# Later waits for loads, wide state reads and a last layer in quarters, in a block-recurrent attention and mixture-of-depths kernel

## The chip, the core and the metric

The kernel runs on one core of one Trainium2 chip. The metric is the time of one execution in microseconds on the device. TensorE (PE) multiplies matrices, VectorE (DVE) and ScalarE (ACT) work element by element, GpSimd (POOL) does small operations and issues the transfers by index, SyncE (SP) issues most other transfers. Each engine works through its own instructions in order.

## What is computed

Eight batches of x (8 heads, 512 rows, 64 columns) and a state (8 heads, 32 rows, 64 columns) attend to each other: every row of x reads the state, every row of the state reads x. The results, 544 rows of 512 columns per batch, go through a mixture of depths: a gate scores each row, and the 128 rows with the highest scores pass a two-layer network.

```python
scores = scale * x @ state.T              # 512 x 32 for each head
xread = softmax(scores) @ state           # rows 0..511 of the output
sread = softmax(scale * state @ x.T) @ x  # rows 512..543
rows = concatenate([xread, sread])        # heads side by side: (8, 544, 512)
s = rows @ w_gate
for b in range(8):
    top = the 128 rows of batch b with the largest s
    ye = maximum(rows[b, top] @ w1, 0) @ w2      # 512 -> 1024 -> 512
    out[b, top] = rows[b, top] + sigmoid(s[b, top]) * ye
```

All data is float32. The profile shows each such matrix product as two records of TensorE.

## The kernel before, in words

**Pieces and their order.** The kernel first writes its work down as 697 numbered pieces (`add`, line 143), each with an engine, a batch and the pieces that it comes after. `carry_out` (line 147) then emits them in the order of the list `ORDER` (lines 18 to 45), which sets the order on every engine at once. An entry `199/0/w04` is piece 199, its PSUM bank 0, and ahead of it 4 dummy products into bank 0 (line 163), whose results nobody reads. All waits follow from buffers and from the dependences written with `add_manual_dep`.

**One batch.** x comes in by rows (`load_x`, line 293, two transfers of 512 KB for batches 1 to 7). Batches 0 to 3 turn x on TensorE (line 411). Batches 4 to 7 also fetch it as blocks in four transfers of 256 KB (`load_x2`, line 309, "blocked x"), which VectorE turns (line 415). The scores are line 448. VectorE works out the softmax over the state (lines 467 to 496). The "read" multiplies it with the state (line 559), in two pieces per batch; each product takes 128 columns of the turned weights in batches 0 to 3 (`WIDE`, line 97) and 64 in batches 4 to 7, hence half as many products when wide. The read also delivers the gate's sums, which VectorE takes out (line 567), while ScalarE copies the rows (line 563). The state's read of x is line 621; batches 4 to 7 get its weights turned over a transfer out (`a_out`, line 587, 512 KB) and four back in (`a_in`, line 592). ScalarE copies its rows (line 627), VectorE makes the state's part of the gate (lines 679 and 689).

**The choice.** A batch's rows are stored to the output (`store_base`, line 646: 1 MB by `store_x`, 64 KB by `store_s`; batch 0 on ScalarE's queue, the others on SP's). The scores, laid out as a row (lines 700 and 703), are compared with each other on VectorE (lines 735 and 742; batches 0 to 2 count the rest on TensorE, line 772). A one-hot matrix (line 788) picks the 128 row numbers (lines 807 and 811). GpSimd then fetches these rows from the output by index ("fetch", line 816), after both stores of the batch have landed. Four to eight small operations give the sigmoid.

**The layers.** They run for the groups [0], [1, 2], [3, 4], [5, 6] and [7] (line 959): the fetched rows are turned (line 874), multiplied with w1 (line 915, "first"), rectified, multiplied with w2 (line 935, "second"), scaled and added to the fetched rows (line 938), and written back by index (`put`, line 946). Batches 6 and 7 do the second layer in two halves of 256 columns (line 929), each with an add and a put of its own; the index of a half is twice the row number plus 0 or 1 (`halved`, line 941).

**What waits behind what.** `HELD` (line 94) makes loads wait until a fetch has landed: x and blocked x of batch 4 behind fetch 0, of 5 behind fetch 2, of 6 behind fetch 3, of 7 behind fetch 4. `HELD_ST` holds batch 1's stores behind fetch 0. `behind` (line 287) writes these waits. Blocked x also comes after the scores of two batches before, and x by rows after the load before it on its queue (`chain`). `touches` (line 638) declares that transfers to the output of different batches do not depend on each other; those of one batch keep their dependence.

Of the kernel before, what the change touches and what calls it, by code (L numbers as in the profile page):

```python
# [10 lines left out]
I32 = mybir.dt.int32  # L11
AF = mybir.ActivationFunctionType
ALU = mybir.AluOpType
# [2 lines left out]


ORDER = """
0 1 2 4 17 3 6 7 8 9 19 20 10 11 31/7/w08 33/6 27/0 35/3 37/2 5 28 32 36 34 38 12 39/0/w03 114/2 40 13 14 116/6 25/5
41/0 45 15 117 26 115 46 47 42 43 16 118/7 29/6 120/2 179/3 181/5 63/4 183/0 65/1 119 121 44 66 180 64 182 24 22 21 54  # L20
500 122/1/w23 185/3 268/7 48 49 123 127 184 269 186 30 67/4 50/5 270/3 52/6 68 51 271 128 129 55/0/w07 175/5 272/4
142/7 124 125 133 71 56 53 126 57 58 273 176 143 72/6 59/0 274/4 275 335 130 73 60 131 132 74/5 144/6 76/7 177/4 75 62
77 178 61 69 145 70 83 187/4/w51 134/0 498/7 146/6 79 81 82 188 135 78 192 80 136 137 499 147 138/0 276/6 141 140 193
194 150 189 139 281 84/2 151/1 85 86 152 198 153/3 207/2 87/5/w01 155/4 209/1 89 154 88 208 156 210 282 283 90 23 91
18 162 190 161 157 160 159 158 277 211/0/w04 333/3 298/2 296/1 96/4 163/7 212 191 92 97 299 334 297 195 196 278 197
279 164 215 165 103/6 98/5 104 99 100 199/0 101 105 166/4 216/7 200 338 341 336 149 337 214 339 148 340 280 201 202
102 167 203/0 106 284 217 285 204 168 286 218/5 220/4 93 170 227 206 219 221 205 108/7 288/0 224 223 225 222 226 228/5
109 107 290 171 291 287 229 230 289 231/6 292/1 300/0 233 232 294 295 301 342 343 94 344 293 345 304 110 307/5 305/1
346/2 306 351 347 213 169 234 95 321 172 235 309/6 240/1 242/0 308 241 243 310 352 353 111 247/4 244/0 253/2 254 248
245 314 348 366 316 311 367 319 318 312 315 317 313 320 349 322 323 302 433 431 434 436 368 435 303 369 324/5 250/6  # L30
350 325 246 255 249 354 326 355 356 251 358/1 370/5 112 437 359 440 357 438 360 361 371 252 236 362/1/w01 374 375/7
363 376 439 327 113 328 237 391 403/0 377/5 379/6 365 378 380 404 364 262/7 441/2 256/5 263 264 432 501 503 373 504
372 506 505 389 238 382 388 387 390 383 381 384 386 385 446 392 393 394/6 257 265 258 259 329 447 448 461 396 462 442
173 443 444 509 510 507 508 463 397 330 174 239 502 464 405/3 445 406 395 511/0 410/6 407/3 408 465/4 449 331 516 512
452 450 451 517 518 409 466 260 531 532 606 607 609 533 608 534 453/0 411 413/4 513 454 514 266 469 455 456 515 457/0
470/5 416/7 414 417 519 520 458 612 471 521 613 522 611 610 332 398 261 486 459 460 415 412 399 418 472/5 474/4 523/0
419/6 535/7 473 475 525 526 536 479 481 478 484 485 483 524 476 480 539 527/0 540/4/w41 528 477 482 541 487 488 530
529 467 468 538 604 537 542/7 544/5/w51 543 545 614/2 489/4 420 421 422 556 400 267 552 553 551 546 555 549 554 548
547 550 557 491 558 619 559/7 490 560 620 621 561 634 401 635 615 625 616 617 423 492 562 402 493 563 425/1 426 427
568/7 570/2 428 636 605 637 569 571 618 494 622 623 429 624 572/7 575/5 573 578/4 626/0 638/6 576 628 564 629 574 639  # L40
627 642 630/0 643/7 579 644 631 632 633 577 495 565 424 659 640 641 645/2 647/6 581/3 598/5 591/0 582 584/7 646 648
580 583 496 651 649 655 653 654 656 652 650 657 658 660 661 566 662/2 585 599 592 600 593 601 586 594 663 567 666 667
497 668 664 669 595 602 665 670 430 590 683 597 603 596 690 671/4 672 587 678/3 673/4 679 674 675 676 680 681 677 682
684/4 685 686 687 691/2 692 693 694 588 688 689 589 695 696
"""


# [1 line left out]
def kernel(  # L49
# [10 lines left out]
    nc = tc.nc  # L60

    B, H, S, D = x.shape
    Ns = state.shape[2]
    Dm, F = moe_w1.shape
    SP = S + Ns
    NC = S // 128
# [25 lines left out]
    XG_BLOCKS = ()  # L92
    TURNED = (0,)
    HELD = {4: 0, 5: 2, 6: 3, 7: 4}
    HELD_ST = {1: 0}
    GATES_PE = (0, 2)
    WIDE = (0, 1, 2, 3)
    ROWS_OUT = ()
    FULL = (3, 4, 5, 6, 7)
    const = pool("const", 1)  # L100
# [2 lines left out]
    small = pool("small", 6)  # L103
# [39 lines left out]
    def add(engine, name, fn, after=(), takes=(), uses=(), b=0):  # L143
        pieces.append(Piece(engine, name, fn, after, takes, uses, b))
        return pieces[-1]
# [80 lines left out]
    after = const.tile([128, SP], F32, name="after")  # L226
# [55 lines left out]
    same_b = ident.bitcast(BF16)  # L282
    xf, p_x, last_load, x2, p_x2, p_scores = {}, {}, [], {}, {}, {}

    fetched = {}

    def behind(b, st):

        for p in fetched.get(b, ()):
            tc.add_manual_dep(st.ins, p.ins.name, mybir.DependencyInfo(mybir.DependencyClass.Sync, mybir.DependencyReason.DATA),  # L290
                              reason="transfers behind the fetch of rows")

    def load_x(b, pieces=2):
        buf = xf[b] = Buf(R_X)
        n = H // pieces
        p_x[b] = []
        for h in range(0, H, n):

            on = "ACT" if b == 0 and h + n == H else "SP"

            def go(h=h, on=on):
                queue = nc.scalar if on == "ACT" else nc.sync
                behind(HELD.get(b), queue.dma_start(out=buf.ap[:, h:h + n], in_=x[b, h:h + n].rearrange("h (p c) d -> p h c d", c=NC)))

            chain = [q for q in last_load if q.engine == on][-1:]
            p_x[b].append(add(on, "load_x", go, after=chain + list(fetched.get(HELD.get(b), ())), takes=[] if h else [buf], uses=[buf] if h else [], b=b))
            last_load.append(p_x[b][-1])

    def load_x2(b):

        buf = x2[b] = Buf(R_X2)
        p_x2[b] = []
        for w in range(2):
            for e in range(2):
                def go(w=w, e=e):
                    src = x[b].rearrange("h (s t r w) (e d) -> w e t r h s d", s=4, t=32, r=2, e=2)[w, e]
                    o = 32 * (2 * w + e)
                    behind(HELD.get(b), nc.sync.dma_start(out=buf.ap[o:o + 32], in_=src))

                p_x2[b].append(add("SP", "load_x2", go, after=[p_scores[b - 2]] + list(fetched.get(HELD.get(b), ())), takes=[] if p_x2[b] else [buf], uses=[buf] if p_x2[b] else [], b=b))  # L320

    def load(on, name, fn, uses=()):
        chain = [q for q in last_load if q.engine == on][-1:]
# [322 lines left out]
    def store_base(b, xs, tmp, p_xs, p_xt):  # L646
        on = "ACT" if b < 1 else "SP"
        queue = nc.scalar if on == "ACT" else nc.sync

        def store(st):  # L650
            touches(b, st)
            behind(HELD_ST.get(b), st)

        def x_rows():
            store(queue.dma_start(out=out[b, 0:S].rearrange("(p c) m -> p c m", c=NC), in_=xs.ap))

        def s_rows():
            dst = out[b, S:SP].rearrange("n (g q d) -> q n g d", g=2, q=4)
            store(queue.dma_start(out=dst, in_=tmp["xt"]))

        held = list(fetched.get(HELD_ST.get(b), ()))
        return [add(on, "store_x", x_rows, after=p_xs + held, uses=[xs], b=b), add(on, "store_s", s_rows, after=[p_xt] + held, b=b)]

    def by_number(b, **kw):

# [194 lines left out]
    def layers(units, number):  # L860
# [4 lines left out]
        n = at[-1]  # L865
        xg, hT = Buf(R_XG), Buf(R_HT)
# [35 lines left out]
        p_h = []  # L902
# [23 lines left out]
        for u, lo in zip(units, at):  # L926
            m, ot = u["m"], Buf(R_OT)

            parts = [slice(0, Dm // 2), slice(Dm // 2, Dm)] if u["b"] >= B - 2 else [slice(0, Dm)]
            for k, part in enumerate(parts):  # L930
                py = Buf(P_H)

# [5 lines left out]
                    nc.vector.scalar_tensor_tensor(ot.ap[0:m, part], py.ap[0:m, part], u["z"].ap[0:m, 2:3], u["xr"].ap[0:m, part],  # L938
                                                   op0=ALU.mult, op1=ALU.add)

                def halved(u=u, m=m, k=k):

                    u[k] = small.tile([128, 1], I32, name="half", bufs=4)
                    nc.gpsimd.tensor_scalar(u[k][0:m], u["idx"].ap[0:m], 2, k, op0=ALU.mult, op1=ALU.add)

                def put(u=u, m=m, ot=ot, part=part, n=len(parts), k=k):
                    ix = u["idx"].ap if n == 1 else u[k]
                    by_number(u["b"], out=flat_out.rearrange("r (n m) -> (r n) m", n=n),
                              out_offset=bass.IndirectOffsetOnAxis(ap=ix[0:m, 0:1], axis=0), in_=ot.ap[0:m, part], in_offset=None)

                p_n = [add("POOL", "halved", halved, after=[u["gate"]], uses=[u["idx"]], b=number)] if len(parts) > 1 else []

                n_parts, p = len(parts), None
                for f0 in range(0, NF, 2):
                    p = add("PE", "second_h" if n_parts > 1 else "second", lambda f0=f0, go=second_layer: go(f0), after=p_h[0:f0 // nf + 1] + [p_w2, p], takes=[] if f0 else [py], uses=[hT] + ([py] if f0 else []), b=number)
                p = add("DVE", "add_h" if n_parts > 1 else "add", add_rows, after=[p, u["gate"]], takes=[] if k else [ot], uses=[py, u["xr"], u["z"]] + ([ot] if k else []), b=number)
                add("POOL", "put", put, after=[p] + p_n, uses=[ot, u["idx"]], b=number)

    groups = [[0], [1, 2], [3, 4], [5, 6], [7]]
# [52 lines left out]
```

## Time and profile before

| What | us |
|---|---|
| median of 3 runs (200.06 to 201.47) | 201.04 |
| the profiled execution | 203.17 |
| its span, first to last instruction | 201.4 |
| TensorE busy | 189.4 |
| VectorE busy | 141.5 |
| ScalarE busy | 77.6 |
| GpSimd busy | 52.2 |
| first layer of group 0 starts | 44.34 |
| first layer of group 1 starts | 70.95 |
| last second-layer product ends | 196.58 |
| batch 1's 1 MB store issued by SP | 51.36 |
| fetch 0, 1, 2, 3, 4 issued | 38.77, 60.13, 63.74, 83.15, 100.24 |
| fetch, issue to landing: least, median, most | 3.4, 4.3, 7.2 |

The profile is of one execution. The span is shorter than the execution's own time, which has start and end around it. TensorE's records end where a model of its pipeline puts them, so durations are best taken from one start to the next. Idle time in brackets names what ended last according to the profile; where that had long been done, it was something else, often a transfer. "issue" is time in which an engine waited for nothing that the profile shows.

### The profile page before, as it was taken

To read this page: it belongs to the slowest core of one execution; us is meant where nothing else is said; L and a number is where in the kernel's file an instruction comes from. 1 tells how busy PE (TensorE), PEld (TensorE's weight loads), DVE (VectorE), ACT (ScalarE), POOL (GpSimd) and SP (SyncE) were. 2 spreads that over 40 slices of the span, in tenths; PEclk is the share of its full clock that TensorE was granted. 3 is DMA by queue.
4 is the path that set the end of the run, shared out by engine and by line. 5 is a ranking of instruction groups with operands and counts; after the bars stand their busy time and mean duration, and the time that the engine had idled before them with its cause. 6 is when DMAs were issued, how large, how long until landed. Compare 5 with 4: busy or idle time off the path is not lost.

```text
span 201.4 us, 5778 instructions
## 1 busy us (share of the span) xinstructions
PE 189.4 (94%) x2412; PEld 138.3 (69%) x2412; DVE 141.5 (70%) x343; ACT 77.6 (39%) x178; POOL 52.2 (26%) x150
## 2 busy tenths in 40 slices
PE   7999999989999799999997999999999999999990
PEld 3787677679956488874444878664468787768980
DVE  4289999999876799758997999699887039011000
ACT  2399886782543412353221452640340451000200
POOL 7020030282414300250022111024620210624042
PEclk9999999999999999999999999999999999999999
DMA  6999946039898498978999988436275051020002
GB/s 193 367 321 373 381 158 226 5 84 180 206 315 312 152 209 191 153 263 144 282 283 151 122 212 138 192 105 277 73 260 88 10 221 49 8 96 26 29 26 78
DMA packets 67218, 35.04 MB, mean 174 GB/s; under 512 B 54904, under 2 KB 63096, under 8 KB 66168
## 3 DMA queue, kind: packets, MB, share of 16 engines
q1 hardware_dynamic: 64676, 28.97, 55.8%
q0 software_dynamic: 1312, 4.20, 6.1%
q10 hardware_dynamic: 1204, 1.51, 2.1%
q8 instruction: 19, 0.31, 0.7%
q14 instruction: 7, 0.06, 0.1%
HBM read 21.56 MB, written 13.11 MB: 172 GB/s over the span
## 4 chain that ended last, share of the span: by engine, by line
PE 56%; DVE 14%; DMA 5%; issue 4%; ACT 2%; POOL 1%; POOLq 1%; DVEq 0%; ACTq 0%
PE ps L915 29%; PE ps L935 15%; PE ps L559 5%; DMA xr<-out_dram,idx 5%; DVE win L742 4%; DVE win L735 3%; PE ps L874 2%; DVE xT L415 2%; PE ps L621 1%; POOL out_dram L666 1%; PE ps L700 1%; DVE oh L788 1%; PE ps L807 1%; DVE spare L583 1%; PE ps L772 1%
## 5 line engine op out<-in xcount | busy, mean ns | idle before, releaser
L915 PE MATMUL ps<-xg,w 128*128 128x256 f32 (+1 forms) x320 | 59.0, 341 | 0.2 <-ACT xg L877 0.2
L935 PE MATMUL ps<-w,hT 128*128 128x512 f32 (+1 forms) x160 | 58.7, 513 | 0.0
L915 PEld LDWEIGHTS ps<-xg,w 128*128 128x128 f32 x320 | 50.6, 191 | 7.0 <-issue 1.4
L935 PEld LDWEIGHTS ps<-w,hT 128*128 128x128 f32 x160 | 29.3, 190 | 19.1 <-issue 17.2
L563 ACT COPY xs<-ps 128x512 f32<-128x512 f32 x32 | 17.7, 590 | 25.6 <-DVE sc L567 11.4
L666 POOL DMA_INDIRECT xr<-out_dram,idx x8 | 9.6, 1194 | 44.1 <-DVE idx L811 21.2
L938 DVE SCALAR_TENSOR_TENSOR ot<-ps,z,xr 128x512 f32<-128x512 f32 (+1 forms) x10 | 6.2, 633 | 20.6 <-PE ps L935 17.7
L735 DVE SCALAR_TENSOR_TENSOR win<-srow,sc,after 128x416 bf16<-128x416 f32 (+4 forms) x40 | 18.9, 506 | 1.9 <-ACT srow L726 1.7
L559 PE MATMUL ps<-st_v,eT 32*64 32x65 f32 (+1 forms) x768 | 18.0, 247 | 1.5 <-issue 0.8
L559 PEld LDWEIGHTS ps<-st_v,eT 32*64 32x64 f32 (+1 forms) x768 | 15.2, 149 | 6.0 <-issue 2.9
L742 DVE SCALAR_TENSOR_TENSOR win<-srow,sc,before 128x512 bf16<-128x512 f32 (+4 forms) x25 | 14.7, 588 | 4.9 <-ACT srow L724 4.5
L918 ACT ACTIVATE hT<-ps 128x512 f32<-128x512 f32 x16 | 9.4, 606 | 15.5 <-PE ps L915 15.5
L484 ACT ACTIVATE e<-e 128x1024 f32<-128x1024 f32 x8 | 8.5, 1060 | 14.7 <-DVE e L481 14.7
L506 ACT ACTIVATE a<-ps,nm 128x512 f32<-128x512 f32 x14 | 9.6, 694 | 9.5 <-DVE nm L502 6.5
L877 ACT COPY xg<-ps 128x512 f32<-128x512 f32 x8 | 4.6, 589 | 17.2 <-PE ps L874 17.1
L163 PE MATMUL ps<-ident 128*128 128x512 bf16 x30 | 9.8, 447 | 1.3 <-POOL ident masks.py:199 1.3
L756 POOL CAST aux<-sc 128x5 bf16<-128x5 f32 x8 | 2.4, 306 | 31.4 <-DVE sc L689 17.8
L415 DVE STREAM_TRANSPOSE xT<-x 128x512 f32<-128x512 f32 x16 | 10.6, 686 | 0.0
L488 DVE TENSOR_REDUCE sm<-e 128x32 f32<-128x1024 f32 x8 | 9.6, 1204 | 0.9 <-ACT e L484 0.8
L502 DVE TENSOR_REDUCE nm<-ps 128x2 f32<-128x1024 f32 x7 | 8.5, 1215 | 2.2 <-PE ps L448 2.2
L493 DVE TENSOR_TENSOR e<-e,sm 128x1024 f32<-128x1024 f32 x8 | 9.7, 1217 | 0.1
L411 PE MATMUL ps<-ident,xf 128*128 128x128 f32 x64 | 9.8, 295 | 0.0
(114 smaller groups left out, 249.4 us busy)
## 6 DMA issues: line engine op xcount, KB each, us to landing
xf<-in_x_dram SPq DMA_DIRECT2D x14, 512.0 KB, 6.0
out_dram<-xs SPq DMA_DIRECT2D x7, 1024.0 KB, 4.9
w<-in_moe_w_dram SPq DMA_DIRECT2D x2, 2048.0 KB
x<-in_x_dram SPq DMA_DIRECT2D x16, 256.0 KB, 4.4
a_d<-spare SPq DMA_DIRECT2D x4, 512.0 KB, 3.8
aT<-a_d SPq DMA_DIRECT2D x16, 128.0 KB, 3.5
out_dram<-xs ACTq DMA_DIRECT2D x1, 1024.0 KB
xf<-in_x_dram SPq DMA_DIRECT2D x3, 256.0 KB
```

Of the source, the lines that this page charges most:

```text
L163: nc.tensor.matmul(banks[:, 512 * bank:512 * (bank + 1)], same_b[:, 0:128], same_b.unsqueeze(1).to_broadcast([128, 2, 256]), start=True, s ...
L411: nc.tensor.transpose(v[:, k, r], xf[b].ap[:, 2 * pair + k, 2 * r:2 * r + 2].rearrange("p w d -> p (w d)"), ident)
L415: nc.vector.transpose(out=t.ap.rearrange("p k r t -> p r k t"), in_=x2[b].ap[:, :, 2 * pair:2 * pair + 2].rearrange("p r k s d -> p r k (s ...
L488: nc.vector.reduce_sum(out=sm, in_=e.ap, axis=AX.X)
L493: nc.vector.tensor_tensor(out=e.ap, in0=e.ap, in1=tmp["sm"].to_broadcast([128, 32, Ns]), op=ALU.mult)
L559: nc.tensor.matmul(view(o)[t, q, c - c0, g], eT.ap[r, c % 2, g, c // 2, t], st_v[r, b, g], start=True, stop=True)
L563: nc.scalar.copy(out=xs.ap[:, c].rearrange("p (g q m) -> p g q m", g=2, q=4), in_=view(o)[:, :, c - c0, :, 0:D].rearrange("p q g m -> p g ...
L666: st = nc.gpsimd.indirect_dma_start(**kw)
L735: nc.vector.scalar_tensor_tensor(wins[c].ap[0:n], srow.ap[0:n, f:SP], sc[0:n, b, c:c + 1], after[0:n, 0:SP - f], op0=ALU.is_gt, op1=ALU.mu ...
L742: nc.vector.scalar_tensor_tensor(unders[c].ap[0:n, 0:f + n], srow.ap[0:n, 0:f + n], sc[0:n, b, c:c + 1], before[0:n, S - f:S + n], op0=ALU ...
L915: nc.tensor.matmul(o, w(j), i[:, :, j] if n == 256 else i[:, 0, j], start=(j == 0), stop=(j == ND - 1))
L935: nc.tensor.matmul(py.ap[0:m, part], hT.ap[:, f, lo:lo + m], w2[:, f, part], start=(f == 0), stop=(f == NF - 1))
```

## The change

Four things are changed, and `ORDER` is a new list for the 711 pieces that result; it has 23 dummies in place of 30.

- The first two blocked pieces of x of batch 4 wait for batch 0's stores to land, and not for fetch 0. In SP's new order batch 1's 1 MB store and batch 2's 64 KB store stand between the two pieces.
- x by rows gets a table of its own (`HELD_X`): batch 4 behind fetch 2, 5 behind fetch 3, 6 and 7 behind fetch 4. It no longer comes after the load before it. Batch 3's stores wait for fetch 2.
- The reads of all eight batches are wide.
- The second layer of batch 7 is done in four quarters of 128 columns, each with its own index, add and put. Batch 6 keeps its halves.

```diff
+    HELD_X = {4: 2, 5: 3, 6: 4, 7: 4}
-    HELD_ST = {1: 0}
+    HELD_ST = {1: 0, 3: 2}
-    WIDE = (0, 1, 2, 3)
+    WIDE = (0, 1, 2, 3, 4, 5, 6, 7)
...
-    fetched = {}
+    fetched, stored, EARLY = {}, {}, 2
-    def behind(b, st):
+    def behind(b, st, of=None):
-        for p in fetched.get(b, ()):
+        for p in (fetched if of is None else of).get(b, ()):
...
-                behind(HELD.get(b), queue.dma_start(out=buf.ap[:, h:h + n], ...
+                behind(HELD_X.get(b), queue.dma_start(out=buf.ap[:, h:h + n], ...
-            p_x[b].append(add(on, "load_x", go, after=chain + list(fetched.get(HELD.get(b), ())), ...
+            p_x[b].append(add(on, "load_x", go, after=(chain if b < 4 else []) + list(fetched.get(HELD_X.get(b), ())), ...
...
+                first_two = b == 4 and len(p_x2[b]) < EARLY
-                    behind(HELD.get(b), nc.sync.dma_start(out=buf.ap[o:o + 32], in_=src))
+                    st = nc.sync.dma_start(out=buf.ap[o:o + 32], in_=src)
+                    if first_two:
+                        behind(0, st, stored)
+                    else:
+                        behind(HELD.get(b), st)
...
-            parts = [slice(0, Dm // 2), slice(Dm // 2, Dm)] if u["b"] >= B - 2 else [slice(0, Dm)]
+            n_parts = 4 if u["b"] == B - 1 else 2 if u["b"] == B - 2 else 1
+            parts = [slice(Dm * k // n_parts, Dm * (k + 1) // n_parts) for k in range(n_parts)]
...
-                    u[k] = small.tile([128, 1], I32, name="half", bufs=4)
-                    nc.gpsimd.tensor_scalar(u[k][0:m], u["idx"].ap[0:m], 2, k, op0=ALU.mult, op1=ALU.add)
+                    u[k] = small.tile([128, 1], I32, name="half", bufs=6)
+                    nc.gpsimd.tensor_scalar(u[k][0:m], u["idx"].ap[0:m], n_parts, k, op0=ALU.mult, op1=ALU.add)
```

SP's transfers after the weights, in both orders (x2 is blocked x, x is x by rows, st the 1 MB store, ss the 64 KB store, ao and ai the way out and back of the weights; the number is the batch):

```
before: x2.4 x2.4 x.4 ss.1 x.4 ss.2 x2.4 st.1 x2.4 st.2 st.3 x2.5 x.5 x2.5 x2.5 ao.4 x2.5 ss.3 ai.4 x.5 x.6
        x2.6 ss.4 x2.6 st.4 x2.6 x2.6 ao.5 x.6 ai.5 x2.7 x2.7 x2.7 ao.6 x2.7 ai.6 st.5 ss.5 ss.6 x.7 st.6 ao.7 x.7 ai.7 st.7 ss.7
after:  x2.4 st.1 ss.2 x2.4 x2.4 ss.1 x2.4 st.2 x2.5 ss.3 x.4 x2.5 x.4 x2.5 ao.4 x2.5 st.3 ai.4 x2.6 x.5
        x2.6 ss.4 x2.6 st.4 x2.6 ao.5 x.5 ai.5 x2.7 x.6 x2.7 x2.7 ao.6 x2.7 x.6 ai.6 x.7 ss.5 st.5 ss.6 st.6 ao.7 x.7 ai.7 st.7 ss.7
```

## The prediction, made before the changed kernel had run

> **What bounds the kernel now.** I read the page's busy shares first, then the 40 slices, the chain that ended last, and then the timelines of the engines and of SP's DMA queue. TensorE is busy in 94% of the span, at a granted clock of 0.999.
>
> ```profile
> PE 189.4 (94%) x2412; PEld 138.3 (69%) x2412; DVE 141.5 (70%) x343; ACT 77.6 (39%) x178; POOL 52.2 (26%) x150
> ...
> PE   7999999989999799999997999999999999999990
> ...
> DMA  6999946039898498978999988436275051020002
> ```
>
> The slices hide two different halves. Up to 44 us VectorE sets the pace (4.1 to 5.0 of each 5 us from 10 on); from 44.34, where the first layer of group 0 starts, to 196.58 PE runs with few holes. These are the holes worth naming, and the reads that the change widens (start, duration, engine; in brackets the idle time ahead):
>
> ```profile
> 57.03 1.12 PE L559 MATMUL ps<-st_v,eT 32*128 32x65 f32 x32
> 58.09 0.69 PE L772 MATMUL ps<-ones,win 128*128 128x1 bf16 x15
> ...
> 68.77 0.63 PE L874 MATMUL ps<-ident,xr 128*128 128x128 f32 x4 [1.49 <-DMA xr<-out_dram,idx]
> ...
> 86.68 0.44 PE L559 MATMUL ps<-st_v,eT 32*64 32x65 f32 x15 [0.40 <-issue]
> 87.06 1.10 PE L621 MATMUL ps<-xf,aT 128*32 128x64 f32 x64
> ...
> 88.56 0.92 PE L559 MATMUL ps<-st_v,eT 32*64 32x65 f32 x64
> 89.41 0.22 PE L686 MATMUL ps<-part_s,same_n 128*32 128x1 f32 x2
> ...
> 107.55 0.63 PE L874 MATMUL ps<-ident,xr 128*128 128x128 f32 x4 [1.07 <-DVE sm L488]
> ```
>
> From start to next start a wide read costs 1.05 us (batches 0 to 3), an undisturbed narrow one 0.85. At 107.55 the last wait is not the VectorE sum: batch 4's row fetch was issued at 100.24 and the longest fetch took 7.2 us to land, so it arrives there. The end of the kernel:
>
> ```profile
> 182.08 1.02 POOL L666 DMA_INDIRECT out_dram<-ot,half  x1 [4.69 <-issue]
> ...
> 184.80 0.97 POOL L666 DMA_INDIRECT out_dram<-ot,half  x1 [1.58 <-DMA out_dram<-ot,half]
> ...
> 189.51 7.07 PE L935 MATMUL ps<-w,hT 128*128 128x256 f32 x32
> ...
> 193.31 0.48 DVE L938 SCALAR_TENSOR_TENSOR ot<-ps,z,xr 128x256 f32<-128x256 f32 x1 [10.00 <-PE ps L935]
> 194.08 1.00 POOL L666 DMA_INDIRECT out_dram<-ot,half  x1 [8.05 <-DVE ot L938]
> ...
> 196.62 0.48 DVE L938 SCALAR_TENSOR_TENSOR ot<-ps,z,xr 128x256 f32<-128x256 f32 x1 [2.82 <-issue]
> 197.38 0.96 POOL L666 DMA_INDIRECT out_dram<-ot,half  x1 [0.90 <-DVE ot L938]
> ```
>
> The reader should see the second line: the second half of batch 6 had been ready, and its put waited for the first half's put to land, 2.72 us from issue to issue. Puts of one batch stay dependent (line 640 frees only other batches).
>
> **The change, part by part.** Sums are against the profiled span of 201.4 us. That execution took 203.17 us, 2.1 above the median of 201.04; I add the difference to the median.
>
> *Quarters.* On PE: two halves take 2 x 3.47 us (189.67 to 193.14); at 128 columns the first layer's rows give 7.14 us for 64 records, 0.112 each, so four quarters of 16 take 7.14: +0.2. On POOL: the changed program's instruction order shows each quarter's put waiting for the landing of the one before. Its PE order interleaves the quarters: quarter 0 is done 9 pieces of 0.447 us, 4.0 us, before PE's end. Add 0.1 of lag, 0.35 for a 128x128 add (estimate from 0.73 at 512 columns and 0.48 at 256), 0.27 from add to put: the first put starts 3.3 us before PE's end. The other quarters are ready every 1.3 us; the puts follow every 2.6 us. Of the 2.72 us the burst of data is some 0.4 (DMA rates of 181 to 186 us), so half the bytes save 0.1 to 0.2; bounds 2.4 (the median landing of a half) and 2.72. The last put starts 3 x 2.6 - 3.3 = 4.5 us after PE's end, where it now starts 0.8 after (197.38 against 196.58). From its start to the span's end it is 4.0 now, 0.1 less with half the bytes. **+3.6** (3.0 to 4.0). The add and the first put are hidden under PE; the rest has no cover, since nothing follows. The two more index multiplications are 0.21 each, in POOL's idle time before.
>
> The Trainium skill, "DMA: Bandwidth & Descriptors", Anatomy of one DMA, gives about 2.0 us fixed, mostly the write receipt, plus bytes over 436 GB/s. By it a 64 KB put would take 2.15 us where a half takes 2.3, and the term would be about 0.4 smaller. It speaks against quarters as the 2.72 row does: what is paid per put hardly shrinks with it.
>
> *Wide reads.* The eight narrow reads of batches 4 to 7 take, start to start, 1.82, 0.85, 1.81, 0.98, 0.85, 0.84, 0.84, 0.84: 8.83. Eight wide ones at 1.05 are 8.40: **-0.4**. This rests on the two slow ones, which stalled on "issue" (0.40 and 0.38, and slow issue around it). I take these as gone, since half of the instructions are left to issue; if they stay (2 x 0.97), the term is +1.5.
>
> The Trainium skill, "TensorEngine Tiling (Array Packing)", Available Configurations, lists eight independent tiles of 32x64 but four of 32x128, which speaks against wide reads; taken alone, with the narrow rows unstalled, it would make them dearer by 8 x 0.20 = 1.6.
>
> *Batch 4's blocked x and batch 1's store.* In SP's queue only one of the two early pieces is early: the second stands behind batch 1's store, which waits for fetch 0 (42.96), and behind the state rows of batch 2. The first moves 256 KB in 35 to 39 us, where the DMA slice is 0, ahead of fetch 0's data. What moves more is batch 1's store: before, it left SP at 51.36 behind six transfers and fetch 1 started only at 60.13, its index ready at 53.9. Now it leaves at 43, so fetch 1 starts at about 54.2 and lands at 59; batch 2's store leaves at about 55.4, lands at 60.4, fetch 2 lands at 65.3 (4.9, as now). PE comes to that row turn at 67.4: the 1.49 idle goes. Next late is the threshold count of batch 2 (VectorE ready 0.4 after PE). PE's own pieces, added up at their rows' times in the new order, come out 0.2 shorter (fewer changes of shape): **-1.3** at the start of group 1's first layer (bounds -1.5 and 0).
>
> *Holding x by rows and batch 3's store behind fetch 2.* Behind the waiting transfer SP now queues st 3, x of 4 and the blocked x of 5, ahead of batch 4's weights (a_out, a_in). Before, from fetch 2's landing (68.7) to a_out's landing (80.0) were 11.3 us for three blocked pieces, one 512 KB piece and a_out. Now another 512 KB (1.35 us at 390 GB/s, seen at 86 to 88) and 64 KB (0.4) are in it, from 65.3: 78.4. Then blocked piece four (1.6), the 1 MB store (2.7 at 60 to 63) and a_in (3.2) give 86 and 0.6 to land. PE needs a_in at 85.8. **+0.8** (0 to 2.5). Fetch 3 now also waits for that store, 83.5, and lands near 88.2; PE wants it at 88.9: hidden, by 0.7.
>
> *Fetch 4.* Its issue stays near 100.2 (store 4 lands at 99.8); one blocked piece fewer runs beside it, so I take 6.0 us to land instead of 7.2 (bounds 4.9, 7.2). PE waits 0.3 instead of 1.07: **-0.8** (-1.1 to +0.4).
>
> *Order.* Batch 1's first gate now stands behind a row copy that follows ScalarE's store issues (1.13 and 0.37): VectorE, the pace up to 44 us, loses **+0.3**. Around 130 to 142 us 0.33 idle and two dummies of 0.45 and 0.49 go, and waits of 0.7 and 0.4 for batch 6's state score and gate come: **-0.3** rounded with the earlier row turn. Seven fewer dummies elsewhere stand in waits and cost nothing.
>
> Sum: 0.2 + 3.6 - 0.4 - 1.3 + 0.8 - 0.8 + 0.3 - 0.3 = **+2.1**, 203.1 us.
>
> **Rivals.**
> A, not slower: every hole goes. From 44.34 to 196.58 PE takes 152.24 us, in it 6.5 of idle, stalls and dummies. Without them, plus 1.6 for wide against unstalled narrow reads and 0.2 for quarters: 147.5. That is -4.7, with the tail +3.6: -1.1, 199.9. For it: fetches lead by 2 us at 67. Against: DMA is full from 70 to 105. It decides once the gain before the last layer passes 3.6.
> B, faster side: the puts do not wait for each other on the chip. Then the last put starts 0.7 after PE's end, the tail term is -0.1, 199.4. With a spacing p the term is 3p - 4.2, so it decides from p below 1.9 on. Against it stands 184.80.
> C, slower: the queue behind fetch 2 is the bound. At the 184 GB/s mean of 70 to 85 us the 3.6 MB up to batch 3's store take 19.6 us from 66.5, until 86.1; fetch 3 lands at 91.2, 2.3 late, and the blocked x of 6 behind it: +4.3, 205.4. It decides when that store lands after 84.
>
> **How the numbers follow.** The forecast has 0.52, C 0.23, A 0.15, B 0.10. Predicted 203.1. Within 1% (what a measurement of this kernel can tell from no change) reaches from 199.0 to 203.05, so the forecast's own spread (201.6 to 204.6) is cut in two: slower 0.27 + 0.23 = 0.50; same 0.25 + 0.13 + 0.05 = 0.43; faster 0.02 + 0.05 = 0.07. The range of 200.0 to 205.6 takes in A's upper side and C, and leaves most of B out.
>
> **What would show it.** Quarters: four puts at the end spaced 2.4 to 2.7 us, each waiting on a DMA, the last starting over 4 us after PE's end; spaced 1.3, B. Reads of batches 4 and 5 at 1.05 without a gap; otherwise that term is wrong. No idle ahead of the second row turn near 67. A wait at L621's state read near 86, and fetch 3 landing before 89; later, C. PE ending near 195; at 192, A.

## The result, and the profile after

The changed kernel takes 213.01 us (median of 4 runs, 211.97 to 214.41), the kernel before on the same chip 201.25 (4 runs): a ratio of 1.059, 95% interval 1.050 to 1.069. The profiled execution took 214.41 us, its span is 212.6 (201.4 before). Ratios, here and below, leave out runs more than 1.5% above the fastest of their kernel; medians do not.

From the page of the changed kernel: TensorE's share and instructions, then 40 slices of 5.3 us of TensorE's busy tenths, of the granted clock and of the DMA engines.

```profile
PE 194.2 (91%) x2181; PEld 142.3 (67%) x2181; DVE 142.6 (67%) x345; ACT 78.3 (37%) x178; POOL 57.3 (27%) x156
...
PE   7997998999999999599999999998999999999910
...
PEclk9999999799999999955999999999999999999995
DMA  6999925357471799959889997743692070102000
```

The clock row was nines throughout before (mean 0.999; now 0.954). It falls in slice 8, in slices 18 and 19, and in the last, where TensorE is idle anyway. TensorE's timeline in the columns of the prediction:

```profile
46.95 3.83 PE L924 MATMUL ps<-xg,w 128*128 128x128 f32 x32
...
70.06 0.60 PE L883 MATMUL ps<-ident,xr 128*128 128x128 f32 x4
...
85.15 1.12 PE L566 MATMUL ps<-st_v,eT 32*128 32x65 f32 x32
...
90.85 1.93 PE L628 MATMUL ps<-xf,aT 128*32 128x64 f32 x64 [2.66 <-DMA aT<-a_d]
...
98.85 8.10 PE L945 MATMUL ps<-w,hT 128*128 128x512 f32 x16
...
114.04 0.60 PE L883 MATMUL ps<-ident,xr 128*128 128x128 f32 x4
```

The first layer of group 0 starts at 46.95 (44.34 before). Batch 2's row turn at 70.06 has no idle ahead, where 1.49 stood. The wide read takes 1.05 from start to next start. Then come the two things to see: batch 4's state read (L628) waits 2.66 us for its weights, and behind it, until 100.8, the clock is at 0.50: that read takes 1.93 instead of 1.10, and 16 matmuls of the second layer, of which a part falls in this time, take 8.10 instead of 7.13. Two stretches of 2 us (busy times, then granted clock, DMA share and GB/s) show hole and clock:

```profile
88.00:90.00 2.00, 0.19 (x1) 0.00 (x0) 0.17 (x1) 0.60 (x1) 0.08 (x1) 1.00 1.02 165
...
92.00:94.00 2.00, 2.00 (x55) 1.83 (x49) 0.30 (x2) 1.01 (x3) 0.00 (x0) 0.50 0.76 122
```

What kept the weights is in SP's own queue (issue time and how long issuing took): x by rows of batch 4, batch 3's store of 1 MB, and only then the weights' way in, which lands at 90.85.

```profile
72.16 2.38 SPq L304 DMA_DIRECT2D xf<-in_x_dram  x1
...
78.55 3.36 SPq L663 DMA_DIRECT2D out_dram<-xs  x1
82.28 4.21 SPq L599 DMA_DIRECT2D aT<-a_d  x4
```

The end, on TensorE, VectorE and GpSimd:

```profile
195.97 6.86 PE L945 MATMUL ps<-w,hT 128*128 128x128 f32 x60
```
```profile
199.01 0.35 DVE L948 SCALAR_TENSOR_TENSOR ot<-ps,z,xr 128x128 f32<-128x128 f32 x1 [10.07 <-PE ps L945]
...
202.88 0.35 DVE L948 SCALAR_TENSOR_TENSOR ot<-ps,z,xr 128x128 f32<-128x128 f32 x1 [0.99 <-PE ps L945]
```
```profile
199.64 1.00 POOL L675 DMA_INDIRECT out_dram<-ot,half  x1 [4.54 <-DVE ot L948]
202.75 0.96 POOL L675 DMA_INDIRECT out_dram<-ot,half  x1 [2.00 <-DMA out_dram<-ot,half]
205.76 0.96 POOL L675 DMA_INDIRECT out_dram<-ot,half  x1 [1.94 <-issue]
208.75 0.96 POOL L675 DMA_INDIRECT out_dram<-ot,half  x1 [1.91 <-issue]
```

All adds are done at 203.2; the puts go on 3.0 us apart, the last one 5.9 us after TensorE's end (0.8 before). Cut at four instructions, the two spans differ like this:

| stretch | before, us | after, us | difference |
|---|---|---|---|
| up to group 0's first layer | 44.34 | 46.95 | +2.6 |
| to group 1's first layer | 26.61 | 25.63 | -1.0 |
| to group 2's first layer | 38.18 | 43.02 | +4.8 |
| to TensorE's last matmul | 87.45 | 87.23 | -0.2 |
| to the span's end | 4.82 | 9.77 | +5.0 |

The sum is the spans' difference, 11.2 us. Both profiles are of long executions, about 2 us above the median before and 1.4 after, so the rows hold to a us or so. Three places need a cause: the start, the middle with the late weights and the half clock, and the end.

### The profile page after: what moved, and what is told of

Same layout as the page of the kernel before. It is cut to its first block, busy times and chain, and to the rows that moved or that the text cites. A ratio compares the mean times of both kernels' runs of the same rounds, so it can differ in the third digit from the quotient of the medians.

```text
span 212.6 us, 5321 instructions
## 1 busy us (share of the span) xinstructions
PE 194.2 (91%) x2181; PEld 142.3 (67%) x2181; DVE 142.6 (67%) x345; ACT 78.3 (37%) x178; POOL 57.3 (27%) x156
## 5 line engine op out<-in xcount | busy, mean ns | idle before, releaser
L945 PE MATMUL ps<-w,hT 128*128 128x512 f32 (+2 forms) x192 | 60.0, 462 | 0.0
L945 PEld LDWEIGHTS ps<-w,hT 128*128 128x128 f32 x192 | 31.0, 193 | 20.2 <-issue 19.1
L675 POOL DMA_INDIRECT xr<-out_dram,idx x8 | 9.5, 1189 | 50.5 <-DVE idx L820 44.8
L744 DVE SCALAR_TENSOR_TENSOR win<-srow,sc,after 128x544 bf16<-128x544 f32 (+4 forms) x40 | 18.9, 508 | 2.7 <-ACT srow L735 2.5
L566 PEld LDWEIGHTS ps<-st_v,eT 32*128 32x128 f32 x512 | 16.6, 194 | 4.1 <-issue 1.7
L566 PE MATMUL ps<-st_v,eT 32*128 32x65 f32 x512 | 18.8, 285 | 0.5 <-ACT xs L570 0.2
L948 DVE SCALAR_TENSOR_TENSOR ot<-ps,z,xr 128x512 f32<-128x512 f32 (+2 forms) x12 | 6.6, 557 | 17.2 <-PE ps L945 17.1
L751 DVE SCALAR_TENSOR_TENSOR win<-srow,sc,before 128x128 bf16<-128x128 f32 (+4 forms) x25 | 14.7, 589 | 3.3 <-ACT srow L733 2.9
L628 PEld LDWEIGHTS ps<-xf,aT 128*32 128x32 f32 x512 | 8.3, 117 | 5.7 <-issue 4.0
L628 PE MATMUL ps<-xf,aT 128*32 128x64 f32 x512 | 9.7, 232 | 2.7 <-DMA aT<-a_d 2.7
L675 POOL DMA_INDIRECT out_dram<-ot,half x6 | 6.0, 997 | 17.3 <-issue 10.7
```

Of the source, the lines that this page charges most:

```text
L566: nc.tensor.matmul(view(o)[t, q, c - c0, g], eT.ap[r, c % 2, g, c // 2, t], st_v[r, b, g], start=True, stop=True)
L628: nc.tensor.matmul(o2.ap[rr, D * g:D * (g + 1)], (aT[g].ap if aT else aT2.ap[:, g])[:, c, rr], xf[b].ap[:, 4 * g + q, c], start=(c == 0), ...
L675: st = nc.gpsimd.indirect_dma_start(**kw)
L744: nc.vector.scalar_tensor_tensor(wins[c].ap[0:n], srow.ap[0:n, f:SP], sc[0:n, b, c:c + 1], after[0:n, 0:SP - f], op0=ALU.is_gt, op1=ALU.mu ...
L751: nc.vector.scalar_tensor_tensor(unders[c].ap[0:n, 0:f + n], srow.ap[0:n, 0:f + n], sc[0:n, b, c:c + 1], before[0:n, S - f:S + n], op0=ALU ...
L945: nc.tensor.matmul(py.ap[0:m, part], hT.ap[:, f, lo:lo + m], w2[:, f, part], start=(f == 0), stop=(f == NF - 1))
```

## The experiments

Each kernel was run beside the kernel before on the same chip; chips differ (medians of the kernel before from 200.9 to 202.6), so the ratio is the number to compare.

| kernel | us | before, us | ratio (95%) |
|---|---|---|---|
| the changed kernel | 213.0 | 201.3 | 1.059 (1.050-1.069) |
| b1: changed, halves | 208.1 | 202.3 | 1.027 (1.019-1.034) |
| c3: changed, puts apart | 207.8 | 202.6 | 1.024 (1.018-1.030) |
| b4: before, quarters | 205.8 | 202.3 | 1.018 (1.008-1.028) |
| a2: changed, store 3 free | 210.3 | 202.1 | 1.045 (1.035-1.055) |
| b2: changed, x of 4 free | 208.5 | 202.3 | 1.029 (1.019-1.039) |
| b3: changed, both free | 208.5 | 202.3 | 1.030 (1.022-1.039) |
| a3: changed, dummies at the late read | 212.7 | 202.1 | 1.052 (1.041-1.062) |
| c2: changed, x of 4 free, halves | 203.0 | 202.6 | 1.002 (0.999-1.006) |
| e1: old order, new transfers, x of 4 free | 201.5 | 201.0 | 1.005 (1.002-1.009) |
| e2: the same, x of 4 held | 204.6 | 201.0 | 1.017 (1.011-1.022) |
| a4: changed, early dummies | 212.8 | 202.1 | 1.057 (1.048-1.066) |
| d1: before, ten dummies fewer | 202.9 | 200.9 | 1.008 (1.004-1.012) |
| c4: the same kernel as d1, 4 runs of 201.4 to 207.6 | 204.9 | 202.6 | not on record |
| d4: changed, x of 4 free, puts apart | 203.5 | 200.9 | 1.006 (1.001-1.010) |
| d2: d4 with the old start | 203.1 | 200.9 | 1.006 (1.002-1.011) |
| c1: before, wide reads | 202.9 | 202.6 | 1.002 (0.998-1.006) |
| d3: c2 without early blocked pieces | 211.9 | 200.9 | 1.053 (1.047-1.059) |

### The end: b1, c3, b4

The theory after the result: holes on TensorE halve its clock, late weights make one hole, serial puts cost 5 us. Its rival: all of it is the queue behind the fetch of batch 2. The edit of b1, with the pieces of the third and fourth quarter out of the order list:

```diff
-            n_parts = 4 if u["b"] == B - 1 else 2 if u["b"] == B - 2 else 1
+            n_parts = 2 if u["b"] >= B - 2 else 1
```

> The changed kernel with batch 7's rows in halves again (two adds, two puts), all else as changed; this time with each step once in the order list. Theory (the serial puts cost the whole difference between the tails, 9.8 and 4.8 us after TensorE's last matmul): 208 us (207 to 209), tail near 5. Rival (the loss lies in the transfers alone): tail near 9, 212 to 213.

```profile
195.36 7.07 PE L945 MATMUL ps<-w,hT 128*128 128x256 f32 x32
```

TensorE ends at 202.43, the span at 207.7: a tail of 5.3 for 9.8, and 1.027 for 1.059. A first try of this (a1) had one piece twice in its list, so that the kernel fell back to program order: 478.3 us. That is what the hand-made order is worth, and nothing on quarters.

> The changed kernel with batch 7's rows in halves again (two adds, two puts), all else as changed. Theory (the changed kernel's loss has three parts: granted clock halved twice behind holes in TensorE's work, the wait of 2.66 us for batch 4's blocked weights, and a longer chain of puts): the tail from TensorE's last matmul to the end goes from 9.8 us back to about 5, so 208 us (207.3 to 208.8). Rival (the whole loss lies behind the transfers that wait for the fetch of batch 2, and the end is hidden as before): the tail stays near 9 us and the time at 212 to 213.

c3 keeps the quarters and takes the wait away:

```diff
-                    by_number(u["b"], out=flat_out...
+                    st = by_number(u["b"], out=flat_out...
+                    for q in u.setdefault("puts", []):
+                        tc.declare_no_dep(st.ins, q.ins, reason="other columns of the same rows")
+                    u["puts"].append(st)
```

> The changed kernel with the puts of one batch's parts declared to be independent (they write other columns of the same rows), so that none waits for the one before. Theory (the tail is the wait of each put for the landing of the last, 3.0 us each): the last put starts right after the last add, the tail goes from 9.8 to about 5.2 us: 208.5 us (207.7 to 209.5). Rival (the chip moves the four puts of 64 KB one after the other anyway): puts about 1.1 us apart, the tail 7 to 9.8, 210.5 to 213.

```profile
200.86 0.96 POOL L675 DMA_INDIRECT out_dram<-ot,half  x1 [0.55 <-POOL z L677]
202.12 0.96 POOL L675 DMA_INDIRECT out_dram<-ot,half  x1 [0.19 <-issue]
203.38 0.96 POOL L675 DMA_INDIRECT out_dram<-ot,half  x1 [0.19 <-issue]
```

The puts come 1.26 us apart, and the tail after TensorE's end (202.38) is 4.9. So the chip overlaps them; the loss was the wait for each landing. b4 has the quarters alone on the kernel before (the change's edit of the parts and of their index; two of the new pieces, 697 and 704, within the old list and 698 to 703 and 705 to 710 behind it, so that one quarter follows the other):

> The kernel before with nothing changed but batch 7's rows put in quarters. Theory: TensorE ends as before (196.6), four puts 3.0 us apart end the run: plus 5 us, 206.3 us (205.5 to 207.2) beside a kernel before of 201.3. Rival 1 (the term as forecast, a pitch of 2.6): plus 3.6, 204.9. Rival 2 (the puts of a row's parts run beside each other): within 1 us of before.

```profile
194.28 0.96 POOL L666 DMA_INDIRECT out_dram<-ot,half  x1 [0.66 <-issue]
197.29 0.96 POOL L666 DMA_INDIRECT out_dram<-ot,half  x1 [1.94 <-issue]
```

Its tail is 8.4 (TensorE ends at 195.78, the span at 204.2): +3.6. The pitch is 3.0 here too. The first put starts 4.5 us ahead of TensorE's end, in the changed kernel 3.2, since that interleaves the quarters: these 1.3 us are the rest of the 5.0. So the 5 us that the theory expected of b4 did not come, and rival 1's number (3.6) came by luck: its pitch of 2.6 did not, and the earlier first put made up for it.

### The middle: a2, b2, b3, c2, e1, e2, a3

```diff
 # a2: and pieces 302, 303 ahead of 433 in the order
-    HELD_ST = {1: 0, 3: 2}
+    HELD_ST = {1: 0}
 # b2: and pieces 336, 337 ahead of 213 in the order
-    HELD_X = {4: 2, 5: 3, 6: 4, 7: 4}
+    HELD_X = {4: 0, 5: 3, 6: 4, 7: 4}
 # b3: both
```

> The changed kernel with batch 3's stores no longer waiting for the fetch of batch 2 and issued by SP ahead of batch 5's blocked x; x by rows of batch 4 stays held. Theory: the store of 1 MB just ahead of the weights' way back is what makes them late; the wait of 2.66 us at 88 goes, and with it the stretch of about 10 us at half clock that follows: 206.5 us (205.5 to 208). Rival 1 (the half clock has another cause than that wait): the wait goes and the clock stays low, 210.3. Rival 2 (the held x by rows, also 1 MB, is enough to make the weights late): the wait stays over 1.5 us and the time over 211.

> The changed kernel with x by rows of batch 4 tied to the fetch of batch 0 again and issued by SP ahead of batch 2's store; batch 3's stores stay held. Theory now (with store 3 out of the way the weights still came at 90.9, so the 1 MB of x by rows that SP issues at 71 to 75, among the blocked x and ahead of the way out, is the larger part): wait at batch 4's state read under 1.2 us, granted clock 1.00 there, group 2's first layer before 111.5 us, 209 us (207.5 to 210.5). Rival 1 (store 3 alone is enough): wait over 2 us, 212 to 214. Rival 2 (the early megabyte delays the fetches of batches 1 and 2): a wait over 1 us at the second row turn near 70, and the time above 211.

> The changed kernel with both x by rows of batch 4 and batch 3's stores no longer behind the fetch of batch 2. Theory (these two transfers together make the late weights): wait at batch 4's state read under 0.5 us, group 2's first layer at 108.5 to 110.3 us against 109.13 before, and the tail's 5 us stay: 207.8 us (206.8 to 209). Rival 1 (only one of them counts): as the better of the runs with one of them free, no more. Rival 2 (the early blocked x, the wider reads or the other order hold the middle up too): group 2's first layer after 111, over 209.5.

```profile
70.97 0.66 PE L883 MATMUL ps<-ident,xr 128*128 128x128 f32 x4 [1.16 <-DMA xr<-out_dram,idx]
...
90.90 1.10 PE L628 MATMUL ps<-xf,aT 128*32 128x64 f32 x64 [1.74 <-DMA aT<-a_d]
```

In a2 the weights came at 90.90, no earlier than at 90.85: the read waits 1.74, and a hole of 1.16 appears ahead of batch 2's row turn. With store 3 ahead of it, the fetch of batch 2 lands later: SP goes on behind it at 70.98 instead of 69.16. From there the weights take 19.9 us instead of 21.7, so the store does count, but freeing it takes away at one end what it gives at the other. This time the clock stays at 1.00, and group 2's first layer starts at 111.42 (115.60 in the changed kernel). My theory, that the store alone makes the weights late, was wrong. b2 frees the x by rows instead: TensorE's timeline,

```profile
86.47 1.10 PE L628 MATMUL ps<-xf,aT 128*32 128x64 f32 x64
...
108.21 0.66 PE L883 MATMUL ps<-ident,xr 128*128 128x128 f32 x4 [2.66 <-DMA xr<-out_dram,idx]
```

The read waits for nothing, and group 2 starts at 109.82. What is late next is the fetch of batch 4, issued at 100.49. b3 gives the same time as b2, so with x by rows free the hold of store 3 costs nothing. c3 is an exception: with both holds its read of batch 4 waits for nothing, since its TensorE, slowed by earlier falls of the clock, comes there only at 93.77. Both repairs in one:

> The changed kernel with x by rows of batch 4 free and batch 7 in halves, both of the runs that helped. Theory (the two losses add: 213.0 minus 4.5 minus 4.9): 203.6 us (202.8 to 205), with the fetch of batch 4 (issued near 100.5, landed near 108) as what group 2 waits for. Rival (the two runs share one gain, since a less loaded chip was measured): over 206.

(The edits of b1 and b2.) 203.0 us, 1.002: the two losses add, and together they are nearly the whole difference. e1 and e2 test the hold outside the changed order: the old list for all engines but SP, halves, wide reads, SP's list of the change. They differ in one entry and in the place of pieces 336 and 337 in SP's list alone:

```diff
 # e2 against e1
-    HELD_X = {4: 0, 5: 3, 6: 4, 7: 4}
+    HELD_X = {4: 2, 5: 3, 6: 4, 7: 4}
```

> The order list of the kernel before for every engine but SP (its matmuls of no use and halves too), with the wide reads and with SP's list of transfers as in the change, x by rows of batch 4 tied to the fetch of batch 0. Theory (group 2 waits for the fetch of batch 4, which lands near 107.5 whatever is gained at 70): as before, ratio 0.994 to 1.004. Rival (the early transfers pay in the old order: the wait of 1.5 us at the second row turn near 69 goes and the gain lasts): ratio under 0.992, which would be a version that beats both.

> The same with one difference: x by rows of batch 4 behind the fetch of batch 2, in the changed kernel's place in SP's list. Theory (the held megabyte alone makes the weights of batch 4 late, in any order): a wait of 2 to 3.5 us at batch 4's state read, in most runs a fall of the granted clock behind it, 3 to 6 us more than the kernel that has it free. Rival (it takes the changed order of TensorE to be hurt): within 1.5 us of it.

e2's timeline:

```profile
86.16 1.10 PE L628 MATMUL ps<-xf,aT 128*32 128x64 f32 x64 [2.20 <-DMA aT<-a_d]
...
91.56 3.48 PE L945 MATMUL ps<-w,hT 128*128 128x512 f32 x4
```

The hold alone costs 3.1 us by the medians (204.55 against 201.45) and 2.3 by the ratios, at or under the low end of what was expected, with the wait of 2.20 and the clock at 0.50 from 88 to 94: four matmuls take 3.48 for 1.98. But one run of e2 at a mean clock of 1.00 took 204.31, between those at 0.978 to 0.983 (204.02 to 205.55; a sixth, at 0.971, took 210.18). So, as far as one run can tell, a fall behind the wait adds little. a3 points the same way; it fills the wait:

```diff
-370/6
+370/6/w612
```

> The changed kernel with 12 matmuls of no use (about 0.21 us each) just ahead of the state read of batch 4 that waits 2.66 us. The wait for the weights itself is not touched. Theory: TensorE is never empty for long there, the granted clock stays at 1.00 from 90 to 101, and about 4 to 5 us of work done at half speed come back: 208.3 us (207 to 210). Rival 1 (the clock falls for another reason than the hole, the wider reads or the transfers): the clock still falls, 213. Rival 2 (the clock's fall costs little, for the engines behind wait for transfers anyway): clock 1.00 and 212 or more.

```profile
89.94 1.10 PE L628 MATMUL ps<-xf,aT 128*32 128x64 f32 x64 [0.86 <-DMA aT<-a_d]
...
111.13 0.66 PE L883 MATMUL ps<-ident,xr 128*128 128x128 f32 x4 [2.12 <-DMA xr<-out_dram,idx]
```

The clock stays at 1.00 from 90 to 110, and the second layer of group 1 starts at 94.52 instead of 98.85. Then TensorE waits for batch 4's rows (issued at 103.88), and the clock falls there, to 0.50 from 112 to 115. The intervals of a3 and the changed kernel overlap: of the 4.3 us gained, 2.1 are spent in this wait, and a part of the rest in the new fall. Rival 2 was right about the time, but not with a clock of 1.00 to the end.

### The start: a4, c4, d1, d2, d4

```diff
 # a4, on the changed kernel
-122/0
+122/0/w03
-55/0
+55/0/w07
 # c4 and d1, on the kernel before
-122/1/w23
+122/1
-55/0/w07
+55/0
```

> The changed kernel with the matmuls of no use that the kernel before had at the scores of batch 1 (3) and the read of batch 0 (7). Theory: the first fall of the granted clock (0.50 from 39.4 to 42.8) comes from thin work on TensorE between 15 and 39 us and goes; group 0's first layer starts near 45 instead of 46.95, and the rest follows: 211.3 us (210.5 to 212.3). Rival 1 (later waits for transfers take it up): first layer near 45, time 212.5 to 213.5. Rival 2 (these matmuls are not what keeps the clock): the clock still falls at 39, time 213.

a4 did nothing (1.057); in its profile, of its longest run, the clock falls at 41.5 all the same, and the first layer starts at 48.62. Ten profiles have the changed kernel's start. In six (a3, b2, b3, c2, d3, d4) there is no fall near 39 and the first layer starts at 44.82 to 45.53; with the fall (the changed kernel, a2, b1) at 46.47 to 46.95. In c3, where the clock was also at 0.50 from 20.1 to 23.5, it starts at 48.46. So 0.9 to 2.1 of the changed kernel's 2.6 us are a fall that comes and goes.

> The kernel before without ten of its matmuls of no use (three ahead of the scores of batch 1, seven ahead of the read of batch 0), which the changed kernel does not have there. Theory 1 (they keep TensorE's work dense enough up to 39 us): the granted clock falls near 39 in about half of the runs, as it did in the changed kernel, and those are 1.3 to 2 us longer: median 202.5 to 203.5 beside 201.5 to 202. Theory 2 (as forecast: they stand in waits and cost nothing): no change, ratio 0.995 to 1.005.

> Once more, in more runs, the kernel before without its ten matmuls of no use at the scores of batch 1 and the read of batch 0: four runs gave 201.4, 202.5, 207.3 and 207.6 us at mean clocks of 1.00, 1.00, 0.98 and 0.975, and no run of the kernel before was under 0.985. Theory 1 (without them the granted clock falls more often): at least a quarter of the runs at a mean clock under 0.985 and 3 us or more longer. Theory 2 (those two were chance): none or one of ten, median within 0.5% of the kernel before.

c4 and d1 are one kernel. Six of its 16 runs had a mean clock under 0.985, none of the 82 runs of the kernel before beside these experiments. Without the four longest runs d1 is still 0.8% slower, 1.6 us. Its profile, two stretches, and the first of them in the kernel before:

```profile
20.00:25.00 5.00, 3.19 (x46) 2.76 (x45) 4.88 (x10) 4.14 (x10) 0.00 (x0) 0.92 1.01 366
25.00:30.00 5.00, 5.00 (x57) 4.43 (x55) 3.61 (x8) 3.49 (x8) 0.91 (x1) 0.73 0.51 195
```
```profile
20.00:25.00 5.00, 4.68 (x55) 3.45 (x54) 4.90 (x11) 4.14 (x9) 0.00 (x0) 1.00 1.00 382
```

TensorE is busy 3.19 us of these five without the dummies, 4.68 with them; the clock goes to 0.92 and 0.73. The first layer starts at 46.01, in the profile of c4, where the clock stayed at 1.00, at 43.50. Where the dummies stood, both have a hole, d1 (the first line) the longer one, and its clock falls 0.9 us behind it:

```profile
23.34 1.20 PE L559 MATMUL ps<-st_v,eT 32*128 32x65 f32 x30 [1.81 <-ACT a L506]
```
```profile
22.09 1.11 PE L559 MATMUL ps<-st_v,eT 32*128 32x65 f32 x30 [1.28 <-ACT a L506]
```

Whether the hole's length or the thin work decides, two profiles don't tell. The dummies stand in waits, but they do not cost nothing to leave out. d4 has the edits of b2 and c3; d2 also has the kernel before's first 205 list entries, dummies too.

> The change with two of its losses mended and its own order list: x by rows of batch 4 tied to the fetch of batch 0, the puts of one batch's quarters independent. Theory (the gains of 4.5 and 5.2 us add): 203.2 us (202.5 to 204.2), as with halves, so quarters bring nothing even where they don't wait. Rival (quarters pay once the puts are apart): under 202.3.

> The change with its three losses mended: x by rows of batch 4 tied to the fetch of batch 0, the puts of one batch's quarters independent, and the order list of the kernel before (its matmuls of no use too) up to the first layer of group 0. Theory (start as before, 43.5 to 44.3 us; no wait at batch 4's state read; a tail of 4.9): 201.5 us (200.5 to 203) beside a kernel before of 202.5. Rival (the fetch of batch 4 holds group 2 whatever comes before): the start is earlier and group 2's first layer is not, 203 us or more.

d4 is at 1.006, d2 at 1.006. d2's first layer starts at 44.72, 0.8 earlier, group 2's at 109.00, 0.7 earlier, behind a wait of 1.70 us for batch 4's fetch; in twelve runs each no gain is left. And quarters brought nothing over halves (c2) even with the puts apart. A little of that lies outside the span: in the profiled runs of c3, d2 and d4, whose puts don't wait, the execution is 2.1 to 2.2 us longer than the span, in the changed kernel and c2 1.8.

### The rest: c1, d3

```diff
 # c1, on the kernel before
-    WIDE = (0, 1, 2, 3)
+    WIDE = (0, 1, 2, 3, 4, 5, 6, 7)
 # d3, on c2: and piece 338 just ahead of 339 in the order
-    fetched, stored, EARLY = {}, {}, 2
+    fetched, stored, EARLY = {}, {}, 0
```

> The kernel before with wide state reads in batches 4 to 7 and nothing else changed. Theory (the term of the forecast: reads of 1.05 us in place of 8.83 us in all for eight, less their pauses): minus 0.4 us where TensorE sets the pace, so 201 to 202 beside a kernel before of 202, ratio 0.995 to 1.003. Rival (the wide reads hold TensorE up, as two more row groups must be loaded): plus 1 or more.

> The changed kernel with x by rows of batch 4 free and batch 7 in halves (203.0 us in ten runs) and now also without the early start of two blocked pieces of x of batch 4: all four behind the fetch of batch 0 again. Theory (the fetch of batch 0 does not mind two pieces of 256 KB, and nothing waits for them): no change, 202.5 to 203.7. Rival (the forecast's term, minus 1.3 us at the start of group 1's first layer, is theirs): 204.3.

c1: no difference (1.002); group 1's first layer starts at 70.97, in the kernel before at 70.95. d3 missed both expectations by 8 us and more:

```profile
65.57 1.12 PE L883 MATMUL ps<-ident,xr 128*128 128x128 f32 x4 [5.58 <-DMA xr<-out_dram,idx]
```

The row turn waits for the fetch of batch 1, issued at 56.86, a few us behind four blocked pieces, 1 MB of x by rows and a 1 MB store (47.3 to 56.8 on SP); the clock is at 0.50 from 61.4, within the hole, to 71.7. In c2 one piece of the four was sent at 35, when the queues are empty, and its row turn, at 59.92, waits for nothing. Whether the bytes or their order delayed the fetch these runs do not tell, nor what the early pieces bring with x of 4 held, which was not run.

No version beat the kernel before. e1 is 2.6 us ahead of it at group 1's first layer (68.37) and then waits for batch 4's fetch (issued at 99.68):

```profile
105.43 0.63 PE L883 MATMUL ps<-ident,xr 128*128 128x128 f32 x4 [2.05 <-DMA xr<-out_dram,idx]
```

At group 2's first layer (107.01) it is still 2.1 ahead of the profile before, which is of a long run, but only 0.8 ahead of c1's (70.97 and 107.82), which has the same wide reads. By that comparison most of what is gained before 70 is spent in this wait, and in its twelve runs e1 is 0.5% slower.

## Why the prediction was wrong, point by point

Three steps failed: the hold behind fetch 2, priced at 0.8, cost 2.3 to 3.1 us on its own (e2 against e1); the pitch of the four puts was 3.0 and not 2.6, so that the tail's term was 5.0 and not 3.6; and the start, priced at 0.3, lost 2.6, of which 0.9 to 2.1 are a fall of the clock that no term had.

- **Quarters, +3.6.** The mechanism was right: four serial puts, the first 3.2 us ahead of TensorE's end (3.3 forecast), the last 3.85 before the end of the span. The mis-sized part is the pitch: 2.6 forecast, 3.0 measured, three times, 1.3 us by the rows; the term was +5.0. The bounds of 2.4 to 2.72 came from halves, with half the data taken to be cheaper. The Trainium skill ("DMA: Bandwidth & Descriptors", Anatomy of one DMA) has a fixed part and a part by bytes, from which I had estimated 2.15 us for 64 KB; no run here shows a put chain that quick. (Three puts at 2.15 in place of 2.6 would have made the term 1.35 smaller, not the 0.4 that I wrote.) The measurement decides: the smaller puts were 0.3 us slower from one to the next, not quicker; why is open.
- **Wide reads, -0.4.** The reads went as forecast (1.05, the two pauses gone). In c1 the time moves by -0.4 to +1.1 us (its interval), so -0.4 cannot be told from nothing, and the +1.5 or 1.6 of the other cases did not come.
- **Batch 4's blocked x and batch 1's store, -1.3.** Right in place and nearly in size: the wait of 1.49 went, -1.0, though with fetch 2 only 0.9 us ahead of TensorE (69.16, 70.06) and not 2.1. I gave the early piece itself little weight; d3 shows that without it, in c2's kernel, fetch 1 costs a hole of 5.58 us.
- **Holding x by rows and store 3, +0.8 (0 to 2.5).** This step failed. The wait was 2.66, and the stretch lost 4.8; with x by rows free (b2: 70.93 to 109.82) it loses 0.7. The chain from fetch 2's landing to the weights was sized well: 65.3 to 86.6 forecast, 69.16 (where SP goes on) to 90.85 measured, 21.3 against 21.7. Its anchor was not: fetch 2 landed 3.9 us late, TensorE came to the read only 2.4 late (88.19 for 85.8). Forecast wait 0.8, plus 1.5 and 0.4, is 2.7. Store 2 left at 58.01 instead of 55.4, as late as the start (2.6); its fetch was issued 7.5 us later, not 5.0, and took 3.7, not 4.9: another 1.2 or 1.3. Of the two held loads the sum gave the store more (2.7 us) than the x by rows (1.35). But b2 and e1, with the store held and x by rows free, have no wait, and a2, with x by rows alone held, still has 1.74.
- **Fetch 4, -0.8.** The wait of 1.07 at the third row turn did go, but by luck, since TensorE came there at 114.04 instead of 107.55; the fetch was issued at 107.81, not 100.2.
- **Order, +0.3, and "Seven fewer dummies elsewhere stand in waits and cost nothing".** This also failed. d1 leaves ten of them out of the kernel before, and that costs 1.6 us. The clock appears in no term of my sum: I had read 0.999 as given, while in c4 and d1 it changes with the work that TensorE has. In the changed kernel the dummies alone don't mend it: a4 has ten of them back and is at 1.057.
- **Rival A** (every hole goes) did not happen: TensorE ended at 202.83, not at 192.
- **Rival C** had the mechanism of the middle, the queue behind fetch 2: it decides when store 3 lands after 84; fetch 3, which waits for that store, was issued at 86.75, and SP went on behind its landing at 91.38, where C had 91.2. But what TensorE waited for was not fetch 3, as C had it (batch 3's row turn at 94.82 has no idle ahead), but the weights. Its price, 2.3 us on top of the forecast, was too small: the stretch lost 4.8 where the forecast had 0.8 and -0.8 in it. C too lacked the start and the pitch.
- **Rival B** (puts don't wait) did not happen, but c3 shows that it was one declaration away; at its spacing of 1.26 its term of about zero is what c3 measured (4.9 against 4.8).

Still open: what part of the start's loss is the clock and what part the order (without a fall the first layer starts at 44.8 to 45.5, in the profiles with the old start, d1 aside, at 43.5 to 44.7), for d2, which puts the order back, shows no gain in time; why the clock falls in some runs of a kernel and not in others; and why fetches of batch 4 take 7 us.

## What to carry to other kernels

A transfer that is made to wait also holds the queue behind it (in the changed kernel SP issues nothing between the store at 58.01 and 69.16): count the bytes from its release to the next transfer that TensorE needs, from a release time that carries every earlier delay of the forecast. Splitting the last stage multiplies whatever each part waits for, so look first whether the parts' writes wait for one another. Matmuls of no use that fill waits may hold the granted clock; before leaving them out, look at how busy TensorE would be without them, and judge by many runs.

## What the hardware showed that I had not expected

The granted clock fell to 0.50 behind holes, but not by their length alone. After 50 us, the profiles here have eleven holes of over 2 us; behind eight the clock fell (2.02, 2.12, 2.13, 2.20, 2.66, 3.29, 3.41 and 5.58 us), behind three it did not (2.05, 2.31 and another of 2.66). Of holes of 1.1 to 1.9 us two in eleven were followed by a fall (1.14 and 1.18). Near 39 us it fell, in four of ten profiles of the same start, with no hole over 0.6 since 20. In d3 it fell at 61.4, 1.4 us after TensorE's last matmul. In the changed kernel it came back after about 3.4 us (39.4 to 42.8) and after about 10 (90.6 to 100.8), with TensorE busy from 90.85 on. The Trainium skill ("TensorE: Matmul & The Clock Gate", Part 1: The HAM clock gate) says that the clock is halved after an idle window of about 3.4 us and that the window runs freely, so that the same kernel differs from run to run. That one kernel differs from run to run agrees with these runs (e2's clock is 1.00 in one and 0.971 in another); that the window runs freely no run here shows. As a safe length of a hole, 3.4 us is too long, as 2.02 shows.

Puts of 64 KB in 512-byte rows that wait for one another are 3.0 us apart, halves of 128 KB 2.72 or 2.73 (in seven profiles); quarters without the wait 1.26.
